# Values in rows of two tokens, keys split into even and odd halves, four score tiles at a time: a change to a windowed attention and token-mixing kernel

## Chip, cores and metric

The kernel runs on one core of a Trainium2 chip. The metric is the device time of one execution in microseconds. Before the change it is 151.2 us (median of three runs, 149.89 to 153.47). Every execution has a state: "slow" is one that is over 1.5% above the fastest of the same kernel.

## The reference

Eight batches of eight heads, 576 tokens, head size 64. Attention looks back over a window of 128 tokens with a distance penalty per head; a token-mixing layer follows.

```python
scores = scale * np.matmul(q, k.transpose(0, 1, 3, 2))          # q, k, v: 8 x 8 x 576 x 64
mask = (rel >= 0) & (rel < 128)                                  # rel = query - key position
scores = np.where(mask, scores + bias[None], -1000000000.0)      # bias = -slope_h * |rel|
attn = softmax(scores)                                           # (written out in the original)
x = (attn @ v).transpose(0, 2, 1, 3).reshape(8, 576, 512)
wq, wk = x @ w_q, x @ w_k
W_tok = scale * np.einsum('bsd,btd->bst', wq, wk)
out = np.maximum(np.einsum('bst,btd->bsd', W_tok, x), 0.0) @ w_out
```

## The kernel before

All work is cut into named operations. A fixed plan gives each its engine and its place; everything is issued in that order, all transfers on SyncE's queue. Scores stand transposed (keys on the partitions, queries along the free dimension). A head pair's scores are made with row tiles of 64 (the head size), ScalarE takes the exponential, VectorE multiplies with a table that holds penalty and mask, and the value products have 128 keys on the partitions:

```python
# loads of v: 128 tokens on the partitions, rows of one token (64 x 4 B = 256 B); 40 issues
nc.sync.dma_start(out=t[0:w], in_=v[b, :, P * kb : P * kb + w, :].rearrange("h s d -> s h d"))

# loads of q and k: nine tokens to a partition, rows of 2,304 B; 32 issues
nc.sync.dma_start(out=t, in_=srcs[x][b].rearrange(
    "(f i a) (g j) d -> f (a g) i (j d)", f=2, a=2, j=9)[f])

# scores: two heads (i) on the two row halves, 128 keys each; 320 products
for i in range(2):
    ps, r = bank(bk[i]), slice(64 * i, 64 * i + 64)
    nc.tensor.matmul(ps[:, a : a + w], kT[b % 2][r, c, P * kb : P * kb + P],
                     qT[b % 2][r, c, P * kb : P * kb + w], start=True, stop=True)

# values: the block before and the own block, 128 keys each; 576 products of 65 columns
# (the 65th is a one that gives the sum)
nc.tensor.matmul(o, p_[:, a : a + P], vt[b % 2][:, t - 1, hv], start=True, stop=False)
nc.tensor.matmul(o, p_[:, a : a + P], vt[b % 2][:, t, hv], start=(t == 0), stop=True)
# ... (start-up, transposes, mixing layer and stores: cut)
```

The softmax here doesn't subtract the row's maximum and nothing guards it: scores larger than these inputs give would overflow.

Of the kernel before, what the change touches and what calls it, by code (L numbers as in the profile page):

```python
# [15 lines left out]
P = 128  # L16
# [83 lines left out]
1G 6D 39S 4D 0G 35S 2D 7D 47S 3G 8P0 5D 43S 14P0 20A 65S 19A 11P0 23A 59S 18A 12P0 17A 61S 24A 25D  # L100
21A 9P0 57S 22A 40A 15P0 53S 26D 13P0 51S 10P0 55S 36A 41P2 73S 42D2 69S 37P0 31S 38A0 48G 33S
250P0 99S 49P2 251A0 44G 245P4 91S 50D2 243P6 77S 244A6 45P0 248P2 66G 46D0 246A4 249A2 67P6 247D
260P0 255P4 261A0 258P2 62G 68D6 60A 253P0 259A2 58D 63P6 252D 64A6 256A4 262D 254A0 52D 54D 56A
257D 85S 403P0 95S 406P2 79S 404D0 74G 405D0 265P4 81S 263P6 266A4 407D2 83S 408D2 411P0 70G 87S
264A6 414P4 412D0 413D0 117S 75P2 32G 71P6 29S 415D4 34G 409P0 416D4 72A6 27S 410D0 113S 417P4
76A2 268P6 100G 418D4 270P0 269A6 280P2 267D 101P4 281A2 273P6 92G 102D4 274A6 531P2 78G 271A0
532D2 278P6 93P4 86G 275P2 279A6 272D 535P0 94A4 96G 533P1 536D0 276A2 534D1 80G 537P4 539P0 277D
111S 97P2 538A4 16P6 125S 98A2 82G 540D0 109S 84G 105S 282D 103S 427P0 419P2 107S 88G 428D0 121S
295P4 420D2 429D0 422P6 296A4 143S 421D2 293P0 118G 89P4 294A0 423D6 424D6 430P2 90A4 431D2 30G
541P0 425P6 432D2 542A0 283P4 426D6 433P2 284A4 28G 288P0 434D2 285P6 286A6 297D 290P4 547P2 289A0  # L110
543P6 287D 545P3 544A6 300P0 114G 546D3 291A4 119P6 548D2 549P3 120D6 301A0 126G 298P4 550A3 115P0
292D 127P6 299A4 650P2 110G 128D6 116A0 645P3 106G 651A2 112G 137S 557P0 646D3 553P4 104G 643P2
139S 554A4 558D0 133S 108G 644A2 135S 302D 435P0 131S 438P2 129S 122G 436D0 310P4 439D2 440D2
648P6 147S 311A4 647S 437D0 303P2 144G 649A6 123P4 304A2 124D4 138G 145P0 446P6 146A0 308P2 140G
447D6 448D6 443P4 309A2 555P0 444D4 441P6 134G 445D4 556A0 141P2 142A2 442D6 449P0 305P4 136G
450D0 306A4 551P6 313P2 552D6 559P0 314A2 132G 307D 315P4 163S 318P6 316A4 320P2 157S 655P1 130G
560D0 151S 319A6 451P4 159S 321A2 663P0 148G 195S 452D4 453D4 177S 323P6 664A0 312D 325P2 165S
149P4 656A1 161S 563P0 324A6 322D 169S 326A2 561P1 155S 317D 652S 454P6 564A0 462P2 150A4 164G
455D6 562D1 653P0 463D2 152G 456D6 459P4 654A0 464D2 660P1 160G 657S 460D4 158G 461D4 173S 153P2
661A1 328P6 189S 154D2 658P0 329A6 196G 203S 330P4 191S 659D0 565P6 333P2 331A4 199S 566D6 178G  # L120
457P0 334A2 465P4 458D0 197P6 466D4 198A6 338P0 166G 571P2 572D2 340P4 339A0 573P6 327D 341A4
575P7 162G 574D6 335P0 569P2 567P4 336A0 170G 577P6 568D4 570A2 576D7 156G 179P0 578D6 167P2 180A0
171P4 332D 467P6 168A2 666P0 337D 172A4 668P1 468D6 469D6 470P2 667A0 669A1 579P4 471D2 581P6
472D2 174G 580A4 673P0 670S 582A6 662S 585P2 342D 175P4 185S 586A2 345P6 671P1 346A6 183S 190G
674D0 181S 478P2 204G 176A4 672D1 187S 348P6 479D2 207S 480D2 475P0 349A6 192G 350P4 476D0 583P2
477D0 351A4 473P6 200G 474D6 481P0 584A2 343P4 482D0 344A4 353P6 355P2 352D 587P0 356A2 683P1
588D0 354A6 347D 678P0 684A1 186G 193P2 679A0 358P4 194D2 360P6 359A4 591P0 184G 361A6 357D 215S
201P2 205P4 209S 202A2 589P1 182G 592D0 221S 681P6 590D1 206A4 217S 188G 211S 362D 491P0 682A6
233S 483P2 225S 492D0 486P4 484D2 216G 493D0 676P6 208G 487D4 485D2 686P7 210G 677A6 488D4 680S
597P0 687A7 370P2 598D0 213S 494P4 371A2 222G 675S 593P6 495D4 373P0 594A6 496D4 241S 489P2 374A0  # L130
229S 380P6 490D2 218G 497P4 665S 498D4 381A6 223P2 375P0 212G 224D2 365P4 237S 376A0 601P6 235S
366A4 603P7 602D6 685S 377D 363P0 239S 599P2 368P4 364A0 605P6 600D2 226G 369A4 604D7 595P0 606D6
234G 227P2 596A0 219P4 372D 378P6 220A4 696P0 214G 228D2 379A6 694P1 697A0 367D 613P4 607P2 609P6
608A2 689P0 610A6 382D 507P2 614A4 691P6 690A0 242G 508D2 509D2 695A1 499P4 230G 692A6 611P0 500D4
383P2 501D4 612A0 693S 502P6 384A2 688S 238G 231P0 503D6 504D6 510P4 232A0 698S 709P2 236G 511D4
512D4 385P0 505P6 386A0 400P4 506D6 701P3 401A4 710D2 240G 398P0 702D3 513P6 711S 399A0 393P4
514D6 699P2 394A4 402D 615P3 700A2 395P0 616D3 388P4 703S 396A0 390P6 387D 617P2 389A4 619P3 618D2
397D 391A6 515P0 706P2 620A3 516D0 392D 621P4 625P6 622A4 704P3 517D0 707A2 626D6 518P4 705A3
627P0 519D4 708S 523P6 520D4 628A0 623P2 524D6 526P0 624A2 525D6 521P4 527D0 528D0 714P2 522D4
529P0 715A2 712P3 530D0 629P2 713D3 631P0 630D2 716S 633P1 632D0 717P0 634A1 639P2 637P4 635P6  # L140
640A2 638D4 641P2 636D6 719P1 642A2 718D0 727P2 720D1 729P3 728A2 721S 724P2 730A3 731S 722P3
725A2 732P2 723A3 726S 733A2 734S
"""

RINGS = {"ld": 8, "ldv": 8, "nat": 6, "vt": 10, "qT": 4, "kT": 4, "P": 4, "x": 8, "xT": 8,
# [97 lines left out]
def steps(nc, pool, pp, q, k, v, moe_w_q, moe_w_k, moe_w_out, out):  # L243
    def sb(shape, dt, name):
        return pool.tile(shape, dt, name=name)
# [8 lines left out]
    ldv = [sb([P, H, D], FP32, f"ldv{i}") for i in range(RINGS["ldv"])]  # L254
    nat = [sb([P, 9, 2, D], F16, f"nat{i}") for i in range(RINGS["nat"])]
    vt = [sb([P, 5, 520], F16, f"vt{i}") for i in range(2)]
    qT = [sb([P, 4, S], F16, f"qT{i}") for i in range(2)]
    kT = [sb([P, 4, 640], F16, f"kT{i}") for i in range(2)]
    pt = sb([P, 4, 2, 1088], F16, "pt")
    table = sb([P, H, 1024], F16, "table")  # L260
# [14 lines left out]
    rel = sb([P, 256], FP32, "rel")  # L275
    reli = sb([P, 256], I32, "reli")
# [21 lines left out]

    def f_iota(eng, bk):
        nc.gpsimd.iota(reli, pattern=[[1, 256]], base=0, channel_multiplier=-1)  # L300

    def f_rel(eng, bk):
        copy(eng, rel, reli)

    def f_mask(eng, bk):
        nc.gpsimd.affine_select(out=rel, in_=rel, compare_op=ALU.is_ge, fill=1.0e9, base=0,
                                pattern=[[1, 256]], channel_multiplier=-1)
        nc.gpsimd.affine_select(out=rel, in_=rel, compare_op=ALU.is_ge, fill=1.0e9, base=127,
                                pattern=[[-1, 256]], channel_multiplier=1)
# [4 lines left out]

    def f_ones(eng, bk):
        for i in range(2):
            nc.vector.memset(vt[i][:, :, 64:520:65], 1.0)
            nc.vector.memset(vt[i][64:128, 4], 0.0)
# [5 lines left out]
    def f_pads(eng, bk):  # L324
        nc.vector.memset(pt[:, :, :, 1024:1088], 1.0)
    op({"POOL": 0.9}, "ident", -99, f_ident, writes=[("ident", 0)])
    op({"POOL": 0.35}, "iota", -98, f_iota, writes=[("iota", 0)])
    op({"DVE": 0.35}, "rel", -97, f_rel, reads=[("iota", 0)], writes=[("rel", 0)])
    op({"POOL": 0.8}, "mask", -96, f_mask, reads=[("rel", 0)], writes=[("mask", 0)])
    op({"DVE": 0.5}, "k zero", -98, f_kzero, writes=[("kzero", 0)])  # L330
    op({"DVE": 0.5}, "ones", -15, f_ones, writes=[("ones", 0)])
    op({"DVE": 0.3}, "zero", -14, f_zero, writes=[("zero", 0)])
    op({"DVE": 0.45}, "pads", -10, f_pads, writes=[("pads", 0)])


    for i in range(9):
        def f_warm(eng, bk):
            for _ in range(4):
                nc.tensor.matmul(bank(bk[0])[:, 0:P], ones, ones, start=True, stop=True)
        op({"PE": 0.45}, f"warm{i}", -98 + i, f_warm, reads=[("ident", 0)],  # L340
           opens=(f"warm{i}", 1))

    for h in range(H):
        def f_exps(eng, bk, h=h):
            nc.scalar.activation(out=table[:, h, 0:256], in_=rel, func=AF.Exp,
                                 scale=-(2.0 ** (-(h + 1))))
        op({"ACT": 0.29}, f"exps{h}", -30 + h, f_exps, reads=[("mask", 0)], writes=[("exps", h)])
    for f in range(2):
        def f_table(eng, bk, f=f):
            t = table[:, 4 * f : 4 * f + 4]  # L350
            for a in range(1, 4):
                w = 256 if a < 3 else 192
                nc.vector.tensor_copy(out=t[:, :, 256 * a : 256 * a + w], in_=t[:, :, 0:w])
            nc.vector.tensor_copy(out=t[:, :, 960:1024], in_=t[:, :, 0:64])
        op({"DVE": 1.15}, f"table{f}", -20 + 2 * f * SLOT, f_table,
           reads=[("exps", 4 * f + h) for h in range(4)], writes=[("table", f)])
# [28 lines left out]
    for b in range(NB):  # L385
# [36 lines left out]
        for kb in range(5):  # L422
# [4 lines left out]
            def f_loadv(eng, bk, b=b, kb=kb, t=t, w=w):  # L427
                nc.sync.dma_start(out=t[0:w], in_=v[b, :, P * kb : P * kb + w, :].rearrange(
                    "h s d -> s h d"))
# [301 lines left out]
```

## Time and profile before

| | before |
|---|---|
| time, span of the profiled run | 151.2 us, 149.7 us |
| TensorE, VectorE, ScalarE busy | 84%, 84%, 79% |
| transfers: packet time of the load and store queue | 88.7% of the span |

The lines that carry these are in the prediction. Two more matter later. On the page (the summary of a profiled run) of the kernel before, the first is a second DMA queue, of kind "instruction" (packets, MB, share), the second the chain that ended last, by engine:

```profile
q8 instruction: 18, 0.29, 0.8%
...
PE 40%; DMA 16%; DVE 13%; ACT 12%; SPq 9%; POOL 4%; issue 2%; POOLq 0%; DVEq 0%
```

18 packets, 0.29 MB: pieces of 16 KB. TensorE has 2,308 products and as many weight loads, 4,616 instructions; 4,616 / 18 is 256 (to the nearest whole number), and in the run `m_fetch` below 18,432 instructions come with 72 pieces, 256 each. So this queue brings TensorE's own program, 256 instructions of 64 B at a time.

### The profile page before, as it was taken

How to read it: one execution, taken by the hardware profiler on the slowest of the kernel's cores; microseconds unless marked ns; L12 is line 12 of the kernel's file. 1: busy time of each engine (PE TensorE's matmuls, PEld its weight loads, DVE VectorE, ACT ScalarE, POOL GpSimd, SP SyncE). 2: the span in 40 equal slices, each digit the busy share in tenths (PEclk: the TensorE clock that was granted, in tenths of full speed). 3: DMA queues.
4: the chain of work that ended last, by engine and by line, in shares of the span. 5: the costliest groups of instructions: out<-in, count | busy, mean ns of one | idle time of the engine just before them, and what ended most of it. 6: DMA issues, size and time to landing. Idle time of an engine off the chain costs nothing.

```text
span 149.7 us, 5314 instructions
## 1 busy us (share of the span) xinstructions
PE 125.7 (84%) x2308; PEld 82.6 (55%) x2308; DVE 125.7 (84%) x212; ACT 118.5 (79%) x170; POOL 58.9 (39%) x78
## 2 busy tenths in 40 slices
PE   6567388676889979889989999999789999999870
PEld 6465167555756456547466566576544757555320
DVE  5749987979999998789999989999799989994700
ACT  6959937995889868997799999959889989741560
POOL 4064137354915767333845381364341710000000
PEclk9999999999999999999999999999999999999999
DMA  4999999999999999999999999799699896033075
GB/s 151 383 327 266 180 365 351 264 171 358 389 263 191 296 299 195 236 306 309 348 348 372 338 405 227 167 254 279 157 371 340 235 385 222 4 140 144 0 314 176
DMA packets 50775, 39.40 MB, mean 263 GB/s; under 512 B 39488, under 2 KB 39488, under 8 KB 50752
## 3 DMA queue, kind: packets, MB, share of 16 engines
q1 hardware_dynamic: 50752, 39.07, 88.7%
q8 instruction: 18, 0.29, 0.8%
q14 instruction: 5, 0.04, 0.1%
HBM read 29.62 MB, written 9.44 MB: 261 GB/s over the span
## 4 chain that ended last, share of the span: by engine, by line
PE 40%; DMA 16%; DVE 13%; ACT 12%; SPq 9%; POOL 4%; issue 2%; POOLq 0%; DVEq 0%
PE bank L159 40%; DMA ld<-in_q_dram 10%; SPq L159 9%; ACT pt L159 8%; DMA ld<-in_k_dram 6%; DVE pt L159 5%; POOL nat L159 2%; ACT qT L159 2%; DVE xT L159 2%; POOL vt L159 2%; DVE x L159 2%; ACT kT L159 1%; DVE kT L159 1%; DVE osb L159 1%; DVE rm L159 1%
## 5 line engine op out<-in xcount | busy, mean ns | idle before, releaser
L159 ACT ACTIVATE pt<-bank 128x1024 f16<-128x1024 f32 x64 | 62.7, 1036 | 9.3 <-PE bank L159 9.0
L159 POOL CAST nat<-ld 128x1152 f16<-128x1152 f32 x30 | 34.2, 1146 | 36.7 <-PE bank L159 10.6
L159 DVE TENSOR_TENSOR pt<-pt,table 128x2048 f16<-128x2048 f16 x32 | 41.0, 1293 | 2.1 <-ACT pt L159 2.0
L159 PE MATMUL bank<-wout_sb,rm 128*128 128x512 f16 x128 | 31.8, 380 | 0.0
L159 POOL CAST vt<-ldv 128x512 f16<-128x512 f32 (+1 forms) x35 | 20.8, 613 | 25.4 <-DVE pt L159 15.5
L159 PE MATMUL bank<-qT,kT 64*128 64x256 f16 (+2 forms) x320 | 25.4, 267 | 4.6 <-ACT qT L159 2.0
L159 PE MATMUL bank<-vt,pt 128*128 128x65 f16 x576 | 23.7, 200 | 4.6 <-ACT pt L159 3.1
L159 PEld LDWEIGHTS <-pt 128*128 128x128 f16 x576 | 21.4, 102 | 9.7 <-issue 2.6
L159 DVE TENSOR_TENSOR x<-bank,inv 128x640 f16<-128x640 f32 x32 | 25.8, 817 | 0.8
L159 PEld LDWEIGHTS <-kT 64*128 64x128 f16 x320 | 14.5, 99 | 11.5 <-issue 8.6
L159 ACT COPY osb<-bank 128x512 f32<-128x512 f32 x24 | 13.9, 606 | 7.1 <-PE bank L159 7.1
L159 PE MATMUL bank<-ident,nat 64*128 64x64 f16 x576 | 14.7, 199 | 5.6 <-POOL nat L159 2.8
L159 PEld LDWEIGHTS <-nat 64*128 64x128 f16 x576 | 12.2, 100 | 10.1 <-POOL nat L159 4.7
L159 PEld LDWEIGHTS <-rm 128*128 128x128 f16 x128 | 10.8, 98 | 12.6 <-issue 2.5
L159 ACT COPY qT<-bank 128x1152 f16<-128x1152 f16 x12 | 13.5, 1121 | 2.6 <-PE bank L159 2.6
L159 ACT ACTIVATE rm<-bank 128x512 f16<-128x512 f32 x21 | 12.7, 610 | 2.2 <-PE bank L159 2.2
L159 DVE COPY kT<-bank 128x1152 f16<-128x1152 f16 x8 | 10.8, 1354 | 3.2 <-PE bank L159 3.2
L159 DVE COPY xT<-bank 128x640 f16<-128x640 f16 (+1 forms) x32 | 12.5, 448 | 0.4 <-PE bank L159 0.4
L159 PE MATMUL bank<-x,wkn 128*64 128x512 f16 x80 | 10.1, 383 | 0.0
L159 PE MATMUL bank<-wqT,gm 64*128 64x256 f16 x64 | 8.4, 288 | 1.5 <-DVE wqT L159 0.6
L159 ACT COPY kT<-bank 128x1152 f16<-128x1152 f16 x8 | 9.1, 1138 | 0.5 <-PE bank L159 0.5
L159 DVE TENSOR_SCALAR rm<-bank 128x512 f16<-128x512 f32 x11 | 7.5, 684 | 2.3 <-PE bank L159 2.2
(45 smaller groups left out, 112.1 us busy)
## 6 DMA issues: line engine op xcount, KB each, us to landing
ld<-in_k_dram SPq DMA_DIRECT2D x16, 576.0 KB, 6.9
ld<-in_q_dram SPq DMA_DIRECT2D x16, 576.0 KB, 7.0
ldv<-in_v_dram SPq DMA_DIRECT2D x32, 256.0 KB, 7.1
out_dram<-osb SPq DMA_DIRECT2D x16, 512.0 KB, 5.2
ldv<-in_v_dram SPq DMA_DIRECT2D x8, 128.0 KB, 7.3
osb<-in_moe_w_out_dram SPq DMA_DIRECT2D x2, 512.0 KB, 7.1
out_dram<-osbt SPq DMA_DIRECT2D x8, 128.0 KB, 3.8
osbt<-in_moe_w_q_dram SPq DMA_DIRECT2D x1, 128.0 KB, 5.3
```

The lines of the kernel that those rows point to most:

```text
L159: r = call(*a, **k)
```

## The change

Its intent: v is loaded in rows of two tokens (512 B); for that the keys of a block are split into even and odd ones, 64 of each, and two heads are stacked on the two partition halves. The score products become four tiles of 64 x 64 that run at a time. At most four transfers are in flight (the two issues of a pair of v loads count as one). The 36 warm-up products go, the start-up tables are built differently, and the plan is drawn up anew.

```diff
 # loads of v: half-height, two issues per pair of heads; 64 (and 16 for the last 64 tokens)
-nc.sync.dma_start(out=t[0:w], in_=v[b, :, P * kb : P * kb + w, :].rearrange("h s d -> s h d"))
+for a in range(2):
+    nc.sync.dma_start(
+        out=t[64 * a : 64 * a + 64].rearrange("p (m w) -> p m w", m=4),
+        in_=v[b, 2 * n + a, 0:512].rearrange("(m p e) d -> p m (e d)", p=64, e=2))
 # scores: 640 products
-nc.tensor.matmul(ps[:, a : a + w], kk, qT[b % 2][r, c, P * kb : P * kb + w], ...)
+for i in range(2):
+    for a in range(2):
+        r, o = slice(64 * i, 64 * i + 64), slice(64 * a, 64 * a + 64)
+        keys = slice(P * kb + w // 256, P * kb + P, 2)
+        nc.tensor.matmul(bank(bk[i])[o, w + c : w + c + n], kT[b % 2][r, 2 * f + a, keys],
+                         qT[b % 2][r, 2 * f + a, P * kb : P * kb + n], start=True, stop=True)
 # values: 1,152 products
+for m, (s, a) in enumerate(terms):          # 4 terms (2 for t = 0), even and odd keys
+    for i in range(2):                      # two heads on the row halves
+        r = slice(64 * i, 64 * i + 64)
+        nc.tensor.matmul(px_of(bk)[:, i, 100 * t : 100 * t + 65], pt[r, c, a : a + P],
+                         vt[b % 2][r, s, c], start=(m == 0), stop=(m == len(terms) - 1))
 # the order of issue
+if o.dma:
+    if len(transfers) >= 4:                 # wait for the transfer four before
+        tc.add_manual_dep(o.insts[0], transfers[-4].insts[-1].name, ..., reason="few")
+    transfers.append(o)
 # ... (tables, mask, memsets, buffers, plan: cut)
```

## The prediction

> **What bounds the kernel now.** The page comes first: busy time of the engines, the transfers, the two biggest groups of work.
>
> ```profile
> span 149.7 us, 5314 instructions
> PE 125.7 (84%) x2308; PEld 82.6 (55%) x2308; DVE 125.7 (84%) x212; ACT 118.5 (79%) x170; POOL 58.9 (39%) x78
> ...
> DMA  4999999999999999999999999799699896033075
> DMA packets 50775, 39.40 MB, mean 263 GB/s; under 512 B 39488, under 2 KB 39488, under 8 KB 50752
> ...
> q1 hardware_dynamic: 50752, 39.07, 88.7%
> ...
> L159 ACT ACTIVATE pt<-bank 128x1024 f16<-128x1024 f32 x64 | 62.7, 1036 | 9.3 <-PE bank L159 9.0
> L159 DVE TENSOR_TENSOR pt<-pt,table 128x2048 f16<-128x2048 f16 x32 | 41.0, 1293 | 2.1 <-ACT pt L159 2.0
> ```
>
> No engine is full, but the DMA row is at 9 for almost 30 of 40 slices, from the second to the last loads. 88.7% of 149.7 us is 133 us of packet time, although 39 MB in 150 us is no large rate. The packets tell why: 39,488 of 50,775 are under 512 B, and 8 x 8 x 576 = 36,864 of these are the rows of v, 256 B each. A window in which v is what lands shows the rate of such rows; the 40 slices of the page show 380 to 405 GB/s where q and k (rows of 2,304 B) move:
>
> ```profile
> 15.00:18.50 3.50, 1.19 (x22) 0.69 (x21) 3.50 (x5) 3.50 (x6) 0.60 (x1) 1.00 1.07 177
> ```
>
> Then the chain of waits in order of time, for what the transfers hold up:
>
> ```profile
> 58.17 6.68 DMA ld<-in_q_dram
> ...
> 100.48 8.88 DMA ld<-in_q_dram
> ...
> 110.72 27.95 PE bank L159 x454
> 138.67 0.02 issue
> 138.69 0.60 ACT rm L159
> 139.29 0.12 ACT rmt L159
> 139.41 0.04 issue
> 139.45 5.61 PE bank L159 x26
> ```
>
> Up to 109 us the chain runs through loads of q and k and through the queue that issues them; the load that lands at 109.4 us feeds the last transposes, and from 110.7 us TensorE works without a gap to 138.7 and, after 0.8 us, to 145. So there are two regimes: loads set the pace until 109 us, TensorE sets the last 40.
>
> **What the Trainium skill says.** "DMA: Bandwidth & Descriptors", Specifications, puts the smallest transfer for line rate at 512 B and has shorter ones do a read-modify-write. The trace agrees on the short side (177 GB/s against some 390); it has no 512 B row. "TensorEngine Tiling (Array Packing)", Key Properties: tiles load weights and multiply in parallel, and a change of tiling mode drains the array. Its Restrictions add that column tiling switches the fast weight load off. "TensorE: Matmul & The Clock Gate", LDWEIGHTS: a load's time goes by its columns, not by its rows. The timeline of TensorE lets me weigh these:
>
> ```profile
> 107.95 0.39 PE L159 MATMUL bank<-qT,kT 64*128 64x256 f16 x4
> 108.17 0.30 PE L159 MATMUL bank<-wqT,gm 64*128 64x256 f16 x2
> 108.46 0.39 PE L159 MATMUL bank<-qT,kT 64*128 64x256 f16 x4
> 108.79 1.27 PE L159 MATMUL bank<-x,wkn 128*64 128x512 f16 x10
> ...
> 110.72 0.70 PE L159 MATMUL bank<-ident,nat 64*128 64x64 f16 x36 [0.42 <-POOL nat L159]
> 111.25 0.38 PE L159 MATMUL bank<-qT,kT 64*128 64x256 f16 x4
> ...
> 114.89 0.71 PE L159 MATMUL bank<-vt,pt 128*128 128x65 f16 x18
> 115.44 1.02 PE L159 MATMUL bank<-wout_sb,rm 128*128 128x512 f16 x4
> ```
>
> From start to start, four score products take 0.22 us when the next work has the same tiling (107.95 to 108.17) and 0.33 when it has not (108.46 to 108.79): a drain is some 0.11 us. 36 transposes on half-height tiles take 0.53 us, 15 ns each; 18 full-height value products take 0.55, 31 ns each. So half-height pairs with 64 columns, each with its own 128-column load, do run two at a time.
>
> **The change, part by part.**
>
> *Loads of v.* Pairs of tokens make rows of 512 B: 18,432 packets for 36,864. I have no row of 512 B to measure; between 177 and 390 GB/s I estimate 320. 9.44 MB / 177 GB/s = 53 us becomes 9.44 / 320 = 30 us: 23 of 133 us of transfer time go. A new rule lets only four transfers be in flight. Four average 1.2 us each in my reckoning (about 110 us over 96 transfers), thus 4.6 us of work against landings of 5 to 7 us that today include the queue; it should hardly starve, and each load lands sooner. The last load, after some 86 us of loads and 11 us of stores, can land at about 99 us instead of 109.
>
> *Values.* With keys split in even and odd halves and two heads stacked, each value product has 64 rows and there are 1,152 for 576. By the transposes above 36 of them take 36 x 15 = 0.54 us, what 18 take now: no gain, no loss.
>
> *Scores.* 640 products of 64 x 64 tiles for 320, four at a time, the same columns streamed. The danger is the weight side: four loads of 64 columns per 256 streamed columns, without the fast load. The plan in the program reckons 0.27 for 0.24 us a group, and 0.56 for 0.54 for values: 64 x 0.03 + 32 x 0.02 = 2.6 us. The order of the instructions has 108 changes of tiling for 95: 13 x 0.11 = 1.4 us. TensorE thus gains 4 us of work; the 36 warm-up products that go (4.0 us busy) stand in time that was idle anyway.
>
> *VectorE and ScalarE.* The order counts 4 evictions of k fewer on VectorE (4 x 1.354 = 5.4 us), 3 rectifications fewer (3 x 0.90 = 2.7), 3 casts of v fewer (1.2), against about 2.5 us more in memsets and tables: 125.7 becomes some 119. ScalarE takes the 4 evictions (4 x 1.138 = 4.6) and 3 rectifications (3 x 0.85 = 2.5), less about 1 us of casts and tables: 118.5 becomes 124.5. The exponentials (64) and the bias products (32) keep number and size.
>
> *Start.* This gets worse. The first exponential starts at 9.86 us now. Ahead of it VectorE gets eight new memsets of 512 or 520 elements (485 ns for 512 today, so 4 us) before it casts the distances; then GpSimd masks in four pieces of 512 (396 ns for 256 today, so about 3 us) and only then casts the first k (1.15 us); ScalarE makes the four tables (about 2 us) before its first eviction. 0.9 + 0.6 + 4 + 0.5 + 3 brings GpSimd to about 9 us, and the cast, the tables and the eviction the first exponential to 12.5: 2.7 us late. Part of that is free, since the first value product waits today until 19.43 us for v.
>
> *Sum.* On ScalarE, the work up to its last exponential is: 64 x 0.93 + 23 evictions x 1.01 + 17 rectifications x 0.62 + 17 half-size copies x 0.49 + 3 casts x 0.6 = 103 us (durations from start to start). Today the same stretch runs from 9.86 to 127.6 us with 100 us of work, 85% full. Without load waits I take 93%: 12.5 + 103/0.93 = 123.3 us. From the last exponential to the end it is 22.1 us today; the tail keeps its chain (bias, values, transpose, mixing, output, store), and the order has 48 output products after the last values for 36, mostly fillers in its gaps: I leave 20.5 to 22. Span 144 to 145. On TensorE: today it needs 125.6 us from 19.4 to 145 for some 107 us of work from start to start; with 111 us, a start about a microsecond earlier and half of the 18.6 us of gaps gone it ends at 18.5 + 111 + 9.5 = 139, plus 4 us of the last copy and store: 143. The two reckonings agree to 2 us, so 144 for the span; times stand 1.5 us above it (151.2 for 149.7): 145.5.
>
> **The rivals.** (a) *Transfers were hidden anyway.* For it: the last 40 us are TensorE's, and chain shares are 40% PE against 16% DMA. Against: TensorE was late in them because loads came late. It would give 149 to 152. (b) *The score tiles are slow*: if four weight loads without the fast path run one after another, a group takes about 0.43 for 0.22 us, 64 x 0.21 = 13 us more on the engine that owns the tail. For it: 64-column loads take 109 ns in the list of groups, 128-column ones 98. Against: the column-tiled ten of 512 columns take 1.21 us (108.79 to 110.0), near 5 x 0.213. With the late start this would give 152 to 156. (c) *Four in flight starve the transfers*, above all v, whose two issues of about 0.5 us each carry 0.8 us of data: loads remain the pace, 147 to 150. (d) *All works and gaps close*: 139 to 141.
>
> **Range and chances.** The middle is 145.5; (c) or half of (a) leads to the upper part, (d) to the lower, so 140.5 to 151.0. The limit of "faster" is 148.2, 2.7 us above my middle: 0.70. Within 2%: 0.22. Slower needs (b) or a much worse start: 0.08.
>
> **What would show it.** Right: packets under 512 B fall to about 2,600; packet time of the queue near 110 us; loads land in 4 to 5 us and the last before 102 us; the first exponential at 12 to 13 us; 36 values in 0.55 us; a score group of eight in 0.25 to 0.30; ScalarE over 92% full from 13 us to its last exponential. Wrong: DMA still at 9 everywhere, score groups over 0.4 us, or ScalarE and VectorE with as many waits for TensorE as now.

## The result

| | before | after |
|---|---|---|
| time, median (lowest to highest, runs) | 152.33 us (149.89 to 156.16, 4) | 170.31 us (168.96 to 173.4, 4) |
| ratio of fast runs | 1 | 1.128 (1.111 to 1.145) |
| TensorE products | 2,308 | 3,168 |
| packet time of the load and store queue | 133 us | 135 us (78.7% of 171.7) |
| first exponential starts | 9.9 us | 14.2 us |
| last exponential ends | 127.6 us | 146.4 us |
| last value product ends | 132.1 us | 151.5 us |

A ratio is the mean time of one kernel's fast runs over that of the other's of the same rounds, so it is not quite the ratio of the medians, in which slow runs count too. The three fast runs of the changed kernel take 168.96 to 170.43 us, 169.9 on average. The change is 13% slower; the prediction had it 4% faster.

The profiled run of the changed kernel fell in the slow state (span 171.7 us; the fast ones have spans of 167.2 to 168.6), so I use its lines for the order of things and test sizes on fast runs. From its page:

```profile
PE 130.9 (76%) x3168; PEld 84.2 (49%) x3168; DVE 125.9 (73%) x211; ACT 124.2 (72%) x176; POOL 71.8 (42%) x84
...
DMA packets 32991, 39.53 MB, mean 230 GB/s; under 512 B 3264, under 2 KB 21696, under 8 KB 32960
...
q8 instruction: 25, 0.41, 1.1%
...
DMA 48%; PE 25%; ACT 12%; SPq 6%; POOL 3%; issue 2%; DVE 0%; ACTq 0%; POOLq 0%
```

ScalarE is as busy as the prediction said (124.2 us for 124.5), and the short rows are gone (3,264 packets under 512 B). But the transfers' share of the chain has tripled, from 16% to 48%. The stretch in which loads set the pace, 2 to 110 us, shows it in one line per kernel (busy time of each engine, granted clock, DMA share, GB/s; first before, then after):

```profile
2.00:110.00 108.00, 91.02 (x1819) 62.84 (x1816) 96.15 (x159) 91.58 (x124) 52.35 (x64) 1.00 1.02 289
```

```profile
2.00:110.00 108.00, 79.87 (x2084) 53.30 (x2086) 85.69 (x140) 81.83 (x108) 58.57 (x66) 0.95 0.97 270
```

The DMA share is about as high as before, but with longer rows the engines move less: 270 GB/s for 289 (276 in a fast run with the same loads and limit, `a_halfpv` below). The times of packets can overlap, so a share near 1 does not prove that no more would go: in `m_rows` below it reaches 1.35. And the chain of waits in order of time (start, duration, what):

```profile
9.69 6.29 DMA ldv<-in_v_dram
15.99 0.60 SPq L158
16.59 0.04 issue
16.63 5.28 DMA ldv<-in_v_dram
...
147.56 18.68 PE bank L158 x215
```

A load lands 5 to 6 us after its issue, only then may the transfer four places later be issued, that takes 0.6 us on the queue, and it again lands 5 to 6 us later. An estimate from these figures: some 89 transfers are issued by the time of the last value product; four at a time, 5.7 us each including part of the issue, they make 89 / 4 x 5.7 = 127 us; the last values came at 151.5. The last line is the tail: 18.7 us of TensorE without a gap.

This looks like the limit of four. So the first theory was: the limit starves the transfers.

### The profile page after: what moved, and what is told of

The parts are those of the page before. It is cut to its first block, busy times and chain, and to the rows that moved or that the text cites. A ratio compares the mean times of both kernels' runs of the same rounds, so it can differ in the third digit from the quotient of the medians.

```text
span 171.7 us, 7143 instructions
## 1 busy us (share of the span) xinstructions
PE 130.9 (76%) x3168; PEld 84.2 (49%) x3168; DVE 125.9 (73%) x211; ACT 124.2 (72%) x176; POOL 71.8 (42%) x84
## 2 busy tenths in 40 slices
DMA packets 32991, 39.53 MB, mean 230 GB/s; under 512 B 3264, under 2 KB 21696, under 8 KB 32960
## 3 DMA queue, kind: packets, MB, share of 16 engines
q1 hardware_dynamic: 32960, 39.07, 78.7%
## 4 chain that ended last, share of the span: by engine, by line
DMA 48%; PE 25%; ACT 12%; SPq 6%; POOL 3%; issue 2%; DVE 0%; ACTq 0%; POOLq 0%
PE bank L158 25%; DMA ldv<-in_v_dram 21%; DMA ld<-in_k_dram 14%; ACT pt L158 6%; DMA out_dram<-osb 6%; SPq L158 6%; DMA osb<-in_moe_w_out_dram 4%; DMA ldvt<-in_v_dram 3%; ACT rm L158 2%; POOL nat L158 1%; ACT osb L158 1%; POOL vt L158 1%; ACT gm L158 1%; ACT kT L158 1%; ACT osbt L158 1%
## 5 line engine op out<-in xcount | busy, mean ns | idle before, releaser
L158 POOL CAST nat<-ld 128x1152 f16<-128x1152 f32 x31 | 37.3, 1212 | 26.8 <-DMA ld<-in_q_dram 8.4
L158 PE MATMUL bank<-qT,kT 64*64 64x256 f16 (+2 forms) x640 | 26.3, 285 | 12.8 <-ACT osb L158 3.7
L158 PE MATMUL bank<-vt,pt 64*128 64x65 f16 x1152 | 26.0, 201 | 7.8 <-POOL vt L158 6.1
L158 POOL CAST vt<-ldv 128x512 f16<-128x512 f32 x29 | 23.0, 806 | 19.2 <-DMA ldv<-in_v_dram 15.7
L158 PEld LDWEIGHTS <-pt 64*128 64x128 f16 x1152 | 23.4, 101 | 12.1 <-issue 9.6
L158 PEld LDWEIGHTS <-kT 64*64 64x64 f16 x640 | 15.9, 120 | 19.6 <-issue 12.2
L158 PEld LDWEIGHTS <-rm 128*128 128x128 f16 x128 | 11.4, 102 | 13.8 <-issue 3.8
L158 ACT ACTIVATE rm<-bank 128x512 f16<-128x512 f32 x24 | 14.9, 630 | 2.6 <-PE bank L158 2.5
L158 DVE RECIPROCAL inv<-bank 128x10 f32<-128x10 f32 x32 | 6.8, 216 | 12.9 <-PE bank L158 12.8
L158 ACT COPY kT<-bank 128x1152 f16<-128x1152 f16 x12 | 13.4, 1127 | 2.1 <-PE bank L158 2.1
L158 DVE CAST wkn<-bank 128x320 f16<-128x320 f32 x8 | 3.9, 491 | 6.1 <-PE bank L158 6.0
```

The lines of the kernel that those rows point to most:

```text
L158: r = call(*a, **k)
```

## The experiments

Four runs or so per kernel. The times are medians of all runs, slow ones among them; the ratio to the kernel before of the same rounds, with its 95% interval, uses fast runs alone. Where times of two runs are subtracted, they are means of fast runs. Theories are named as they were then: "starvation" is the limit of four, "I" the many half-height issues, "F" TensorE waiting for its own instructions.

### Is it the limit of four?

`a_nolimit`, the changed kernel without the rule:

```diff
-            if len(transfers) >= 4:
+            if False:
```

> The changed kernel without the rule that a transfer waits for the fourth one before it; nothing else differs (the eight transfer semaphores still bound what is in flight). Theory 1, the rule starves the loads: 170 us falls to 145 to 150 us, the mean rate over the span rises from 227 to some 265 GB/s, and the transfer waits in the chain shrink from 48% to under 25%. Rival 2, the rows of 512 B in pairs of half-height transfers are what is slow: it stays above 163 us. Rival 3, the order of the plan (loads queued behind stores that wait for results) is what is slow: it stays above 163 us too, with the queue's waits for the output copies at 25 us or more.

172.17 us, 1.147 (1.124 to 1.170). Not faster: two of the four runs are slow, and the fast ones, 170.1 and 170.9, are as long as the changed kernel's. `a_limit6` has `>= 6` and `transfers[-6]`:

> The changed kernel with six transfers in flight in place of four. Theory 1: between the two, some 152 to 160 us. Rivals 2 and 3: 168 to 171 us, as with four.

172.41 us, 1.144 (1.130 to 1.159). `b_limit4` is the kernel before with the rule:

> The kernel before with the rule of four transfers in flight added, nothing else. Theory 1: the rule alone makes it slower, 160 us or more. Rivals 2 and 3: it stays within 2% of the kernel before, 149 to 154 us, since neither rows nor order are touched.

152.78 us, 1.016 (1.009 to 1.024). So the rule by itself costs 1.6%, and taking it from the changed kernel brings nothing. Starvation as the sole cause falls. (`b_limit4` also warns of reading a cost from the chain: transfers have 63% of its chain, more than the 48% of the changed kernel, and it loses 1.6%.) But without the limit the chain is another: TensorE has 50% of it, "issue" 14%, and transfers are gone from it. The timeline of TensorE without the limit (fast run; start, duration, work, and in brackets the idle time before it and what ended it) says why:

```profile
33.16 0.30 PE L158 MATMUL bank<-qT,kT 64*64 64x256 f16 x3
37.07 0.58 PE L158 MATMUL bank<-qT,kT 64*64 64x256 f16 x5 [3.61 <-issue]
```

One operation of eight score products stops after the third for 3.6 us, with nothing that it waits for. In that run such stops stand at instructions 702, 958, 1470, 1980, 2236, 2492, 2748, 3002 ... (the one at 2236 falls between two operations): at multiples of 256 plus about 190. Eleven of them make 16.9 us, counted from the start of one product to that of the next. In the kernel before there are two, 1.7 us; with six in flight (`a_limit6`) they still make some 16 us. Each ends 1.3 to 1.8 us after one of the 16 KB pieces of the instruction queue has landed. This is theory F. The skill has a section on it that I had not read before predicting: "Runtime: NRT & Kernel Launch", Instruction fetch mechanics, says that an engine's instruction memory is refilled in 16 KiB blocks of 256 instructions through a DMA queue of its own, and calls the cost of crossing a boundary mostly hidden. The block size agrees with the 25 pieces for 6,336 instructions; that it is hidden does not.

### The transfers alone

`m_rows` runs the loads of v in both forms and those of q, each without and with the limit, and nothing else (zeros as output; core of it):

```python
for make, limit in ((v256, 0), (v512, 0), (q2304, 0), (v256, 4), (v512, 4), (q2304, 4)):
    phase(make(), limit)        # v512: the two half-height issues of the changed kernel
```

> A measurement, wrong result on purpose (the output is all zeros): transfers alone, in six phases one after the other: all of v in rows of 256 B, all of v in rows of 512 B as the changed kernel loads it, all of q in rows of 2,304 B, with eight transfer instructions in flight, then the same three with four transfers in flight. Theory 1: rows of 512 B move at 300 GB/s or more with eight in flight, 256 B at 180 to 220, and with four in flight each form loses 20% or more. Rival 2: rows of 512 B in half-height pairs move at less than 250 GB/s even with eight in flight.

Two stretches (no engine works; the last two columns are the DMA share and GB/s), first rows of 256 B, then half-height pairs of 512 B:

```profile
2.00:45.00 43.00, 0.00 (x0) 0.00 (x0) 1.00 1.35 211
50.00:100.00 50.00, 0.00 (x0) 0.00 (x0) 1.00 0.65 185
```

The rows of 512 B are slower as they are loaded here, 185 for 211 GB/s, and the DMA engines are only 65% busy: what limits them is the issue, some 0.65 us for each 128 KB. q runs at 392 GB/s. With four in flight the rates are 217, 182 and 391, so the limit harms none of them here. My 320 GB/s falls.

### TensorE's instructions by themselves

`m_fetch` (zeros): 9,216 half-height products of 65 columns that wait for nothing, in six stretches of 1,536, each beside other transfers.

```python
for make, limit in ((None, 0), (q2304_and_k2304, 0), (v256, 0), (v512, 0),
                    (q2304_and_k2304, 4), (v256, 4)):
    for n in range(1536):                      # 12 x 256 instructions
        r = slice(64 * (n % 2), 64 * (n % 2) + 64)
        nc.tensor.matmul(banks[n % 2][:, 0:65], w_[r], m_[r], start=True, stop=True)
    # the transfers of a stretch start with its first product
```

> TensorE's instructions measured by themselves; the outputs are zeros on purpose. TensorE runs six stretches of 1,536 half-height products of 65 columns without any wait (12 times 256 instructions each), first with no transfer in flight, then beside rows of 2,304 B, of 256 B, half-height pairs of 512 B, 2,304 B with four in flight, 256 B with four in flight. If TensorE's instructions come in pieces of 256 that queue behind the data (theory F), the stretch alone takes some 2 to 3.5 us per 256 instructions, those beside unlimited loads 4.5 to 6 us with a stop of one to several us at every 256th instruction, ending about 1.4 us after a piece lands, and those with four in flight lie between. If the stops come from something else in the kernel (order, score banks, clock), all stretches run at about 2 us per 256 (15 ns a product) and no stop is periodic.

TensorE's timeline, three blocks with nothing else in flight, then one beside loads in rows of 2,304 B:

```profile
13.98 2.12 PE L88 MATMUL bank<-m__99,w__98 64*128 64x65 f16 x128 [1.61 <-issue]
...
36.90 3.70 PE L88 MATMUL bank<-m__99,w__98 64*128 64x65 f16 x128 [1.14 <-issue]
40.91 2.33 PE L88 MATMUL bank<-m__99,w__98 64*128 64x65 f16 x128 [0.30 <-issue]
...
86.63 3.71 PE L88 MATMUL bank<-m__99,w__98 64*128 64x65 f16 x128 [2.49 <-issue]
```

Every 128 products (256 instructions) there is a stop, with or without data in flight. The granted clock is no rival for it. It was 0.5 from 34.6 to 41.4 us and from 68.7 to 96.0, and there 128 products took 3.7 us instead of 2.1. But with nothing in flight the slow block (36.90) was followed by a stop of only 0.30 us, and from start to start it took 4.0 us, like its neighbours: the period is that of the refill, not of the products. The table has the time of each stretch, divided by its twelve blocks:

| beside | us per 256 instructions, mean of the stretch |
|---|---|
| nothing | 3.7 |
| rows of 2,304 B | 5.4 (6.2 while the loads are at full rate) |
| rows of 256 B | 4.3 |
| half-height pairs of 512 B | 3.9 |
| rows of 2,304 B, four in flight | 5.0 (4.8 to 6.5 from the fifth block on; before, the half-height loads of the last stretch still ran) |
| rows of 256 B, four in flight | 4.6 |

All 69 stops of over 0.3 us end 1.2 to 1.65 us after a piece lands. The products themselves take some 17 ns at the full clock; the refill allows 29 ns for a product and its weight load when alone (3.7 us / 128) and up to 48 beside loads. So two half-height products at 15 ns, which replace one full-height product at 31 ns, are not the same to TensorE: they use up instructions twice as fast as these arrive. The expectation was half right: the periodic stop is there, but already without data, and the limit of four hardly helps.

### More instructions in the kernel before

`b_morepe`: the kernel before, its loads and its plan untouched, but each score and value product cut in two, so that TensorE has about as many products (3,204) as in the changed one. The result stays correct.

```diff
-nc.tensor.matmul(ps[:, a : a + w], kk, qT[b % 2][r, c, P * kb : P * kb + w], ...)
+for half in range(2):
+    r, o = slice(64 * i, 64 * i + 64), slice(64 * half, 64 * half + 64)
+    nc.tensor.matmul(bank(bk[i])[o, a : a + w], kT[b % 2][r, c, k0 : k0 + 64], ...)
 # values likewise: 64 of the 128 queries in each of two column tiles
```

> The kernel before with its own loads and order, but TensorE's work cut into as many instructions as in the changed kernel: scores as four 64 x 64 tiles (640 for 320), values as two column tiles of 64 queries (1,152 for 576). The result stays right. Theory F: stalls 256 instructions apart grow from 2 us to 10 or more, and the time rises by 6 us or more, to 158 or above. Theory I, or an order that does not fit: under 156 us, unless the value products themselves get longer (36 in much over 0.6 us).

167.09 us, 1.105 (1.096 to 1.114); stops of 12.9 us, where the kernel before has 1.7. The cut products are also a little longer (36 value products 0.69 us for 18 in 0.65, eight score products 0.345 for four in 0.315), some 3 us in all by my estimate; the stops are the larger part of the 16 us. The same with the rule of four, `b_morepe_limit4`:

> The kernel before with as many TensorE instructions as the changed one (167.1 us alone), plus the rule of four transfers in flight (which alone costs 1.6% on the kernel before). Theory F with refills queueing behind data: the stops shrink from 13 us to about 5, the time falls to 159 to 165 us unless the loads become the wait. If the refills do not queue behind data: stops as large as before, 168 to 171 us.

164.54 us, 1.091 (1.079 to 1.103), stops 7.2 us. TensorE is also busier here than in the changed kernel (133.6 us in the last run, for 130.9), so these are not exact copies of its load; but cutting products alone makes the kernel before some 10% slower.

### Fewer instructions in the changed kernel

`a_halfpv_nolimit`: no limit, half the value products, each streaming two blocks (130 columns), so that the streamed work stays and the instructions go (wrong result; for the last tokens there is one block of 65). `a_halfpv` is the same with the limit of four.

```diff
-for m, (s, a) in enumerate(terms):
+for m, (s, a) in enumerate(terms[::2]):
-    nc.tensor.matmul(px_of(bk)[:, i, 100 * t : 100 * t + 65], pt[r, c, a : a + P], vt[b % 2][r, s, c], ...)
+    nc.tensor.matmul(<two blocks of 65>, pt[r, c, a : a + P], <vt[b % 2][r, s, c] twice>, ...)
```

> Wrong result on purpose: without the limit, half the value products, each streaming the same 65 columns twice, so about the same streaming with 1,152 fewer TensorE instructions (576 products and their weight loads). Theory F: the stalls shrink from 14 us to 7 or less and the time falls by 6 to 12 us, to 160 to 166. Theory I and an order that does not fit: 169 to 173 us.

162.41 us, 1.076 (1.068 to 1.083): 8.2 us less than with all products. The stops fall from 16.9 to 6.5 us; a group of value products also takes 0.57 us for 0.65, some 2.6 us in 32 groups.

> The changed kernel with half the value products, each streaming two blocks (wrong result on purpose), the limit of four and the half-height loads of v kept. If under the limit the loads set the pace and hide the instructions: 166 to 170 us. If TensorE's instructions count by themselves there too: 158 to 163 us, as without the limit (162.4).

168.72 us, 1.122 (1.113 to 1.131): with the limit only 1.1 us less. So in the changed kernel as it is, the instructions are not what sets the pace.

### One issue for a pair of v loads

`a_onev_nolimit` and `a_onev` load the two heads of a pair with one transfer over all 128 partitions: the same bytes, rows of 512 B, half the issues (the small loads of the last 64 tokens stay cut). The tokens that land are the wrong ones: the right ones need an access pattern of four dimensions, and the build refused it ("Unable to balance aps with more than 3 dims").

```diff
-for a in range(2):
-    nc.sync.dma_start(out=t[64 * a : 64 * a + 64]..., in_=v[b, 2 * n + a, 0:512]...)
+nc.sync.dma_start(out=t.rearrange("p (m w) -> p m w", m=4),
+    in_=v[b, 2 * n : 2 * n + 2].rearrange("a s d -> (a s) d")[0:1024].rearrange(
+        "(m p e) d -> p m (e d)", p=128, e=2))
```

> Wrong result on purpose (v of the wrong tokens): without the limit of four, each pair of half-height loads of v is one load of full height, 32 fewer issues, same bytes in the same rows of 512 B. Theory I, the issues of half-height loads hold up the queue: 172 us falls to 155 us or less. Theory F, TensorE stands still while it waits for its own instructions (stalls in the middle of an operation, 256 instructions apart, 14 us of them without the limit): the stalls stay and the time stays above 165 us.

167.38 us, 1.108 (1.099 to 1.117), stops of TensorE still 15.2 us.

> The changed kernel with its limit of four, but each pair of v loads issued as one transfer over all partitions (wrong v on purpose, same bytes and rows of 512 B). Without the limit this was worth 5 us (172.2 to 167.4). If under the limit the loads of v, two issues each, are what sets the pace: 158 to 163 us and the loads of v leave the chain. If the stops of TensorE set the pace here too: 166 to 169 us.

156.80 us, 1.041 (1.032 to 1.050): 13.4 us less than the changed kernel, more than either theory had said. The stretch from 2 to 110 us in this run:

```profile
2.00:110.00 108.00, 84.65 (x2381) 56.70 (x2383) 92.80 (x155) 91.43 (x123) 60.79 (x76) 1.00 0.98 312
```

312 GB/s for 270 (slow run; 276 in the fast `a_halfpv`) at the same DMA share. The chain has no transfers left (TensorE 48%, ScalarE 16%, issue 14%). An issue takes 0.37 us (median) for all 128 partitions and 0.61 for half of them; a 512 B packet takes 28.5 ns on average for 34.5, and the packets of q and k beside it 112 for 124 (34.4 and 122 in the fast `a_halfpv`). Packet time of the queue falls from 135 to 121 us. The skill had said it: "DMA: Bandwidth & Descriptors", Rules for kernel authors, of two transfers to disjoint partition halves: "Use one 128-partition transfer".

### Half-height loads in the kernel before

`b_split` cuts each load of v of the kernel before into its two partition halves, rows of 256 B kept; the result stays correct.

```diff
-nc.sync.dma_start(out=t[0:w], in_=v[b, :, P * kb : P * kb + w, :].rearrange("h s d -> s h d"))
+for a in range(2):
+    r = slice(w // 2 * a, w // 2 * a + w // 2)
+    nc.sync.dma_start(out=t[r], in_=v[b, :, P * kb + r.start : P * kb + r.stop, :].rearrange(...))
```

> The kernel before with each load of v cut into two half-height transfers, without a limit. If half-height transfers cost mainly by themselves (more packet time, 40 more issues): 157 to 165 us, near the 164.3 with the limit. If they cost only under a limit, where each landing is waited for: 151 to 155 us.

163.02 us, 1.081 (1.069 to 1.094), packet time 143 us for 133. Half-height loads cost by themselves, without limit, without many instructions. With the limit, `b_split_limit4`:

> The kernel before with the limit of four (152.8 us) and each load of v cut into two half-height transfers, as the changed kernel has them, rows of 256 B kept. If two half-height issues under a limit of four are a cost of their own (13.5 us in the changed kernel): 158 to 166 us, and loads of v take a large share of the chain. If they only cost together with the many TensorE instructions: 152 to 156 us.

164.32 us median, but three of its four runs are slow (163.9 to 168.4) and the one fast run is 159.84, so there is no ratio; that the limit makes cut loads dearer is not shown. And with the many instructions as well, `b_morepe_split_limit4`:

> The same with as many TensorE instructions as the changed kernel (164.5 us without the cut loads): the slowdown rebuilt from the side of the kernel before. If the two causes are the whole story: 168 to 178 us, with stops of TensorE under 8 us, near the changed kernel's 170.3. Below 165 us: the half-height issues are not what the run with one issue took away, but something of that run's layout.

167.44 us, 1.099 (1.085 to 1.112), the profile from a slow run. That is a little below the range that I had set (168 to 178). Two of its four runs are slow; the fast ones take 165.6 us on average, 4.3 less than the changed kernel, and the second cause adds only 1.7 us to the first (163.9). They overlap.

### All taken away

`a_start` moves the cast of the distances ahead of two groups of memsets (two entries of the plan swap places), because the first exponential is late:

```diff
-1G 4D 22S 6D 5D 26S 0G 2D 46S ...
+1G 2D 22S 4D 6D 26S 0G 5D 46S ...
```

> The changed kernel with one difference of order on VectorE: the cast of the distances and the slopes stand ahead of the memsets, not behind them. The first exponential starts 14.2 us after the start in the changed kernel and 9.9 in the kernel before. If the late start is carried to the end, the time falls by about as much as the first exponential moves (4 us, to 166 us); if the loads set the pace anyway, it stays at 170.

169.68 us, 1.114 (1.101 to 1.126). The first exponential starts at 11.4 us for 14.2. Two of the four runs are slow; the fast ones take 168.0 us on average, 1.8 less, but the intervals of the two ratios overlap, so a gain is not shown. `a_all` has the one-issue loads, half the value products and the early cast, no limit; `a_all_limit4` the same with the limit (wrong results):

> All suspects out at once: the changed kernel without the limit of four, with v in one issue per pair, half the value products (each streaming two blocks), and the distances cast before the memsets (wrong result on purpose). If the three parts add up (172.2, less 4.8 for the issues, less 9.8 for the instructions, less 1 for the start): 155 to 158 us, with stops of TensorE under 9 us. If they overlap, 160 us or more.

153.66 us, 1.024 (1.016 to 1.031).

> The changed kernel with one issue per pair (156.8 us), half the value products and the early cast of the distances, the limit of four kept (wrong result on purpose). If the remaining 4% over the kernel before are TensorE's instructions and the late start: 149 to 152 us. If 154 to 157: something else of the change, such as the score tiles, is left.

155.76 us, 1.025 (1.012 to 1.039), two of four runs slow. 2.4% over the kernel before are left. In the profile of `a_all` the last exponential ends at 126.4 us and the last value product at 131.4, both earlier than before (127.6, 132.1); but from there to the end it takes 19.4 us for 17.6. So the rest shows in the tail, where the plan leaves 48 output products after the last values for 36. That the score tiles cost nothing is not shown by this: the value groups of `a_all` are shorter than those of the changed kernel.

### A try at a better version

`b_warm9`, the kernel before with 9 warm-up products for 36 (`range(1)` for `range(4)`), fewer instructions:

> A try at a version better than both: the kernel before with 9 warm-up products instead of 36, 54 TensorE instructions fewer. Its stops for instructions are only 1.7 us, so 150 to 151.5 us, the same within 1%; if the clock is not granted as early, up to 153.

151.52 us, 1.007 (0.999 to 1.016): the same. I found no version that beats the kernel before.

### The runs in one table

Means of the fast runs in us (two to four each, in rounds whose kernel before took 150.3 to 150.9); "cut" are half-height loads of v.

| changed kernel | limit of four | no limit |
|---|---|---|
| as it is: cut, 1,152 value products | 169.9 | 170.5 |
| one issue | 156.4 | 167.4 |
| half the value products | 168.8 | 162.3 |
| both (and early cast) | 154.5 | 153.5 |

With the limit the cut loads set the pace: taking them away is worth 13.4 us, the instructions 1.1 (with loads in one issue 1.9, early cast included). Without the limit the instructions come first: 8.2 us for them, 3.1 for the loads. The changed kernel carries two handicaps. In the kernel before each alone costs most of the 13% (8.1% the cut loads, 10.5% the instructions); in the changed one it depends on the limit which of them is felt. That is why neither removing the limit nor removing instructions alone seemed to help.

## Why the prediction was wrong

**What bounds the kernel** was right in part. The DMA share is near 1 until about 110 us before and 125 us after, and cut loads alone cost 8%. But faster loads did not pay as it thought: see the sum.

**Loads of v: this step failed.** It put rows of 512 B at 320 GB/s and took 23 of 133 us of packet time away. Packet time went to 135 us. A 512 B packet had a median of 27 ns (mean 34.5) for 18 (19.8) of 256 B. Summed over 16 engines the rows of v took 39.7 us for some 45.5: 6 us saved, and given back by slower packets of q, k and the stores beside them (q and k 63.5 us for 58.2). The 53 us that the step started from came from the rate of one window; the packets of v themselves had 45.5. Alone, the pairs run at 185 GB/s. The step looked at the row length only. That a load was now two half-height issues stood in rival (c), "two issues of about 0.5 us each carry 0.8 us of data", and was priced at 147 to 150 us: the direction was right, the size was not (13.4 us by `a_onev`, 8% by `b_split`).

**The limit "should hardly starve".** Right for the transfers alone (`m_rows`) and for the kernel before (1.6%). But the working set 4.6 us of transfer time against a landing that would shrink. The landing stayed at 5.3 to 6.1 us, and with half-height issues it became the pace.

**Values, "no gain, no loss".** The 36 products do take 0.55 us from start to start. What is missing in the sum is a term: TensorE's instructions have to arrive. Twice the products in the same time need twice the refill, which gives 29 to 48 ns per product and weight load against 15 needed. Shown by `m_fetch`, `b_morepe` and `a_halfpv_nolimit`. In the changed kernel as it is, this is mostly hidden behind the loads.

**Scores.** Near enough: seven stretches of three groups of eight products, undisturbed by waits, took 0.59 to 1.08 us up to the next work, median 0.78, so 0.26 us a group for the 0.25 to 0.30 that it asked for. Rival (b), 0.43 us a group, did not happen. Of what it quotes on weight loads, the traces agree that rows do not count (64 rows 100 ns, 128 rows 102); that columns do is not shown: loads of 64 columns took 109 to 120 ns for 93 to 104 with 128, but they are column tiles too.

**VectorE and ScalarE.** ScalarE was right, VectorE 125.9 us for 119 (122.4 in the fast `a_all`); neither decides here, since both wait more.

**Start.** 12.5 us predicted, 14.2 measured; that moving it to 11.4 gains anything is not shown.

**Sum.** "93% full" between first and last exponential was the sum's main assumption, and it needed the loads to get out of the way. `a_all` shows what that is worth. Its packet time is 119 us for 133 and both handicaps are out, and ScalarE is busy for 91% between its first and last exponential, near the 93 assumed (87% before). Yet the last exponential comes only 1.2 us earlier, since the first comes 1.5 us later and ScalarE has 2.6 us more to do in between, and the time is 2.4% above the kernel before. So no run here shows that longer rows make the whole faster, and rival (a), 149 to 152 us, comes closer to this run (153.5) than the middle of the prediction. The tail was also mis-sized: 20.5 to 22 us after the last exponential, 25.3 measured (25.2 in the fast `a_nolimit`). The twelve more output products, 12 x 0.22 us = 2.6 us, were taken as fillers of gaps; there are none.

**What stays open.** Why a half-height issue takes 0.61 us and one over all partitions with twice the bytes 0.37, no run shows; nor why packets beside half-height loads are slower. Cutting a load halves its height and doubles the issues at once; two issues over all partitions were not tried, so the two are not told apart. The limit of four goes with fewer stops (7 us for 15 with one issue, 0.6 for 6.5 with half the value products), but in `m_fetch` it hardly speeds the refill, so whether it protects the instructions or only slows TensorE below their rate is open.

## What to carry to other kernels

A longer row was worth nothing here, since the transfer was cut to half the partitions to get it: measure the transfer as it will be issued, with its issue time, before counting on its row length. Count TensorE's instructions as well as its columns, above all where products on half-height tiles take 15 ns each, and look for "issue" stops in the middle of operations, 256 instructions apart. When removing a suspected cause changes nothing, another bound may stand right behind it: remove the suspects together as well as one by one.

## What the Trainium skill lacked or had wrong

- "Runtime: NRT & Kernel Launch", Instruction fetch mechanics: it calls crossing a 16 KiB boundary mostly hidden. With half-height products TensorE stopped at every boundary: 3.7 us per 256 instructions with nothing else in flight, up to 6.2 us beside loads in rows of 2,304 B, single stops up to 4.8 us, each ending 1.2 to 1.8 us after a piece landed. Cutting the products of the kernel before in two cost 10.5%.
- "DMA: Bandwidth & Descriptors", Specifications, puts line rate at 512 B and up. The row length alone did not give it here. Half-height loads with rows of 512 B ran at 185 GB/s with the DMA engines 65% busy, rows of 256 B over all partitions at 211, rows of 2,304 B at 392.
- "DMA: Bandwidth & Descriptors", Rules for kernel authors, advises against two transfers to partition halves but gives no price: 0.61 us per issue for 0.37, 512 B packets of 34.5 ns for 28.5, and 8.1% of the whole kernel's time (`b_split`).
